# Zeroing a cache gradient: one zero region split between a memory-to-memory copy and a store, and one zero store issued earlier

## The chip, the cores and the metric

The kernel runs on one core of one Trainium2 chip. The metric is the device time of one execution in microseconds (us); lower is better. Five engines work side by side in a core: PE (TensorE, matrix multiplication), DVE (VectorE), ACT (ScalarE), POOL (GpSimd) and SP (SyncE). SP computes nothing; here it issues nearly all transfers. Transfers are carried by the core's 16 DMA engines, each of which works through its own share of every transfer, in the order in which SP issued them.

## What is computed

It is the forward pass and all gradients of a small decoding block: four tokens, one attention layer that looks at the last 1024 positions of a 4096-position key and value cache, and a feed-forward layer, added together. Cut to what matters here:

```python
def _A_ref(x, k_cache, v_cache, wq, wo):
    W = min(4096, max(256, Sk // 4))            # 1024
    k = jnp.repeat(k_cache[:, :, Sk - W:, :], rep, axis=1)
    v = jnp.repeat(v_cache[:, :, Sk - W:, :], rep, axis=1)
    scores = jnp.einsum("bhqd,bhkd->bhqk", q, k) * (Dh ** -0.5)
    o = jnp.einsum("bhqk,bhkd->bhqd", _softmax(scores), v)
    ...
return x + _A_ref(xn, ...) + _B_ref(xn, ...)    # and its vjp with grad_out
```

The outputs are the result, the gradient of x, the gradients of the two caches (`out_2` for keys, `out_3` for values, each 4 x 8 x 4096 x 128 in bf16) and the gradients of the five weight matrices. Only the last 1024 of the 4096 positions of a cache take part, so the first 3072 positions (`K0`) of both cache gradients are zero. They still have to be written: two tensors of 4 batches x 8 kv-heads x 3072 x 128 x 2 bytes, 768 KB for each kv-head, 48 MB in all.

## The kernel before

The kernel loads the feed-forward weights, does the feed-forward forward and backward passes, and then goes through the attention in four groups `t` of two kv-heads each (`NT` = 4). A group loads its part of the two caches and of the two attention weights, builds scores and probabilities (`kv_steps`, `softmax`, `softmax_d`), and leaves behind gradient pieces: `stg_dv` and `stg_dk` for the caches (1 MB each, two of each in a group), `osb_o` and `osb_q` for the weights (512 KB each, two of each in a group). The pieces (functions `dvdk` and `dw`) are put in a list `bg`, and `tick` takes them out between the matrix multiplications of the main line, so the pieces of group t are made while group t+1 runs. Each piece ends in a call of `store` (line 100), which puts one DMA on SP's queue.

The zeros come from `ztile`, a tile in on-chip memory (128 rows of 12 KB) that is set to zero once. `zlist` (line 159) holds 32 regions, each of two neighbouring kv-heads of one batch of one tensor; the last one belongs to `out_3`. `zero(n)` (line 161) takes the next n of them and stores `ztile` to each: 1.5 MB in 128 rows of 12 KB. Calls of `zero` are strewn over the program by hand: after the cache-gradient stores (line 490), after some of the feed-forward stores, at the start of the attention part, and a batch of four in the last group (line 734). What is left in the list when all is issued is stored at line 755.

SP issues everything in program order and stands at each DMA until what it stores has been written by DVE or ACT. Besides, a DMA waits until the one eight places before it in the order has landed, since eight completion semaphores are used in turn. `store` says that gradient stores and zero stores write disjoint bytes, so they don't wait for one another on that ground. The tiles that hold gradient pieces are used in turn too: three of the kind `stg`, four of the kind `osb`; DVE and ACT can only refill one when its last store has landed.

Of the kernel before, what the change touches and what calls it, by code (L numbers as in the profile page):

```python
# [14 lines left out]
P = 128  # L15
# [3 lines left out]
def kernel(  # L19
# [28 lines left out]
    nc = tc.nc  # L48

    B, Sq, D = A_x.shape  # L50
    _, G, Sk, Dh = A_k_cache.shape
# [4 lines left out]
    K0 = Sk - W  # L56
    F = B_w_gate.shape[1]
    ND = D // P
    NF = F // P
    GP = 2  # L60
    NT = G // GP
# [27 lines left out]
    def evac(out, in_, n, half=False, eng=None):  # L89

        eng = "dve" if half else eng
        ca, cd = (190 + n) / 1.2, (120 + (n / 2 if half else n)) / 0.96
        if eng is None:
            eng = "act" if load["act"] + ca <= load["dve"] + cd else "dve"
        load[eng] += ca if eng == "act" else cd
        if eng == "act":
            return nc.scalar.copy(out=out, in_=in_)  # L97
        return nc.vector.tensor_copy(out=out, in_=in_)  # L98

    def store(eng, out, in_, kind):  # L100

        eng.nop()
        d = eng.dma_start(out=out, in_=in_)
        for k in ("rest", "zeros") if kind == "rest" else ("rest",):
            tc.declare_no_dep(d.ins, group=k, reason="stores write disjoint parts of the outputs")
        tc.add_to_no_dep_group(kind, d.ins)
        return d
# [12 lines left out]
    def load_w(t, eng=nc.gpsimd):  # L120
        pool = w_pool[t % 2]
        wo_t[t] = pool.tile([P, HG, D], BF16, name="wo_sb", tag="wo")
        eng.dma_start(out=wo_t[t][:], in_=wo_v[t])
        wq_t[t] = pool.tile([P, ND, CW], BF16, name="wq_sb", tag="wq")
        eng.dma_start(out=wq_t[t][:], in_=wq_v[t])
# [32 lines left out]
    ztile = const.tile([P, ZW], BF16, name="ztile")  # L158
    zlist = deque((og, b, g) for b in range(B) for g in range(0, G, ZR) for og in (out_2, out_3))

    def zero(n=1):
        for _ in range(min(n, len(zlist))):
            og, b, g = zlist.popleft()
            store(nc.sync, og[b, g:g + ZR, 0:K0, :].rearrange("g (m j) d -> m g (j d)", m=P // ZR), ztile[:], "zeros")


    nc.gpsimd.memset(ztile[:], 0.0)
# [94 lines left out]
    def tick(n):  # L262
        for _ in range(min(n, len(bg))):
            bg.popleft()()
# [3 lines left out]
    def link(n=1):  # L268
        for _ in range(min(n, len(chain))):
            chain.popleft()()  # L270
# [227 lines left out]
    def dw(t):  # L498
        o_s, dq_r = st[t]["os"], st[t]["dq"]

        def piece_o(g, i, held):
            if i == 0:
                held["osb"] = outp.tile([P, rep, D], BF16, name="osb_o", tag="o")
            mps = ps_w.tile([P, D], FP32, name="dwo_ps", tag="w")
            nc.tensor.matmul(mps[:], lhsT=o_s[:, g].rearrange("p r d -> p (r d)")[:, i:rep * Dh:rep], rhs=dyr[:],  # L505
                             start=True, stop=True)
            evac(held["osb"][:, i, :], mps[:], 512)
            if i == rep - 1:
                r0 = (t * HG + g * rep) * Dh
                store(nc.sync, out_5[r0:r0 + rep * Dh, :].rearrange("(p i) n -> p (i n)", i=rep),  # L510
                      held["osb"][:].rearrange("p i n -> p (i n)"), "rest")

        def piece_q(c2, k, held):
            if k == 0:
                held["osb"] = outp.tile([P, 2, GP, rep, Dh], BF16, name="osb_q", tag="o")
            ci, i2 = k // 2, k % 2
            c = c2 * 2 + ci
            mps = ps_w.tile([P, 2, GP, Dh], FP32, name="dwq_ps", tag="w")
            for i in range(2):
                nc.tensor.matmul(mps[:, i].rearrange("p g d -> p (g d)"), lhsT=xnm[:, i2 * 2 + i, c * P:(c + 1) * P],  # L520
                                 rhs=dq_r[:].rearrange("p g d -> p (g d)"), start=True, stop=True)
            evac(held["osb"][:, ci, :, i2 * 2:(i2 + 1) * 2, :], mps[:].rearrange("p i g d -> p g i d"), 512)
            if k == 3:
                store(nc.sync, out_4[c2 * 2 * P:(c2 + 1) * 2 * P, t * CW:(t + 1) * CW].rearrange("(c p) j -> p c j", p=P),
                      held["osb"][:].rearrange("p c g i d -> p c (g i d)"), "rest")

        assert rep == 4
        made = []
        for g in range(GP):
            held = {}  # L530
            made.append([lambda g=g, i=i, held=held: piece_o(g, i, held) for i in range(rep)])
        for c2 in range(ND // 2):
            held = {}
            made.append([lambda c2=c2, k=k, held=held: piece_q(c2, k, held) for k in range(4)])
        return made
# [181 lines left out]
    with tc.tile_pool(name="kv_b", bufs=GP, reuse_waits="tile") as kv_b, \  # L717
            tc.tile_pool(name="w_b", bufs=1, reuse_waits="tile") as w_b, \
            tc.tile_pool(name="stage", bufs=3, reuse_waits="tile") as stage:
        kv_pool[1], w_pool[1] = kv_b, w_b  # L720
        zero()
        pre(0)
        load_w(1)
        load_kv(1, 0)
        for t in range(NT):
            kv_steps(t, 0, 0)
            if t == 0:
                zero()
                load_kv(1, 1)
                zero()  # L730
            softmax(t)
            kv_steps(t, 1, 1)
            if t == NT - 1:
                zero(4)
            link(len(chain))
            softmax_d(t)
            link()
            odq(t, 0)
            load_kv(t + 2, 1)
            if t + 1 < NT:  # L740
                pre(t + 1)
            link(len(chain))
            odT(t, 0)
            odq(t, 1)
            load_kv(t + 2, 0)
            tick(2)
            odT(t, 1)
            fin(t)
            if t + 2 < NT:
                load_w(t + 2)  # L750
            (k0, k1), (o0, o1, q0, q1) = dvdk(t, 1), dw(t)
            for p in (k0, o0, k1, o1, q0, q1):
                bg.extend(p)
        tick(len(bg))
        zero(len(zlist))

        fin_ps = []
        for o in range(2):
            f_ps = ps_w.tile([B, ND, P], FP32, name="f_ps", tag="w")
            for c in range(ND):  # L760
                nc.tensor.transpose(f_ps[:, c, :], acc[:, o, c, :], ident_f[:])
            fin_ps.append(f_ps)
        acc_o = fin_ps[0][:].rearrange("b c p -> b (c p)")
        acc_d = attw.tile([B, P, ND], FP32, name="acc_d", tag="P_s")
        nc.vector.tensor_copy(out=acc_d[:].rearrange("b p c -> b c p"), in_=fin_ps[1][:])
        acc_d = acc_d[:].rearrange("b p c -> b (p c)")
        out_b = attw.tile([B, D], BF16, name="out_b", tag="pT")
        nc.vector.tensor_tensor(out=out_b[:], in0=acc_o, in1=x4[:], op=ALU.add)
        nc.scalar.dma_start(out=out_0.rearrange("b s d -> (b s) d"), in_=out_b[:])

        s1 = attw.tile([B, 1], FP32, name="s1", tag="m")
        nc.vector.reduce_sum(out=s1[:], in_=acc_d, axis=AX.X)
        pr = attw.tile([B, D], FP32, name="pr", tag="dS_s")
        s2 = attw.tile([B, 1], FP32, name="s2", tag="es")
        nc.vector.tensor_tensor_reduce(out=pr[:], in0=acc_d, in1=xn_f[:], scale=1.0, scalar=0.0,
                                       op0=ALU.mult, op1=ALU.add, accum_out=s2[:])
        nm1 = attw.tile([B, 1], FP32, name="nm1", tag="rr")
        nc.vector.tensor_scalar(out=nm1[:], in0=s1[:], scalar1=-1.0 / D, scalar2=None, op0=ALU.mult)
        nm2 = attw.tile([B, 1], FP32, name="nm2", tag="gs")
        nc.vector.tensor_scalar(out=nm2[:], in0=s2[:], scalar1=-1.0 / D, scalar2=None, op0=ALU.mult)  # L780
        nc.vector.scalar_tensor_tensor(out=pr[:], in0=xn_f[:], scalar=nm2[:, 0:1], in1=acc_d,
                                       op0=ALU.mult, op1=ALU.add)
        nc.vector.tensor_scalar(out=pr[:], in0=pr[:], scalar1=nm1[:, 0:1], scalar2=rstd[:, 0:1],
                                op0=ALU.add, op1=ALU.mult)
        dx_b = attw.tile([B, D], BF16, name="dx_b", tag="E_f")
        nc.vector.tensor_tensor(out=dx_b[:], in0=pr[:], in1=dy4[:], op=ALU.add)
        nc.scalar.dma_start(out=out_1.rearrange("b s d -> (b s) d"), in_=dx_b[:])
# [30 lines left out]
```

## Time and profile before

| | |
|---|---|
| median of 3 runs | 282.91 us (282.87 to 283.6) |
| the profiled execution, its own time | 283.0 us |
| span of that execution in the profile | 281.0 us |
| busy: PE / DVE / ACT / POOL | 203.1 / 164.1 / 117.8 / 40.1 us |
| moved by DMA | 112.12 MB, 30.68 MB read from memory and 81.01 MB written |
| zero stores | 32 of 1536 KB, 18.1 us from issue to landing in the middle |
| `stg_dv` and `stg_dk` stores | 8 and 8 of 1024 KB, 13.0 and 20.8 us to landing |

The span runs from the first to the last recorded event of the core; the time of the execution is 2.0 us longer. "Busy" is the time in which an engine had an instruction in work. In a table by stretches of time, the column "DMA share" gives the mean busy share of the 16 DMA engines: 1.00 is all of them all the time (it can read a little over 1 where neighbouring packets overlap in the records), and 0.06 is one of them alone. "From issue to landing" counts from SP's instruction until the last of a transfer's bytes is in place, so it holds the time that the transfer stands behind earlier ones.

### The profile page before, as it was taken

How to read it: one execution, taken by the hardware profiler on the slowest of the kernel's cores; microseconds unless marked ns; L12 is line 12 of the kernel's file. 1: busy time of each engine (PE TensorE's matmuls, PEld its weight loads, DVE VectorE, ACT ScalarE, POOL GpSimd, SP SyncE). 2: the span in 40 equal slices, each digit the busy share in tenths (PEclk: the TensorE clock that was granted, in tenths of full speed). 3: DMA queues.
4: the chain of work that ended last, by engine and by line, in shares of the span. 5: the costliest groups of instructions: out<-in, count | busy, mean ns of one | idle time of the engine just before them, and what ended most of it. 6: DMA issues, size and time to landing. Idle time of an engine off the chain costs nothing.

```text
span 281.0 us, 6867 instructions
## 1 busy us (share of the span) xinstructions
PE 203.1 (72%) x2972; PEld 138.8 (49%) x2972; DVE 164.1 (58%) x313; ACT 117.8 (42%) x219; POOL 40.1 (14%) x40
## 2 busy tenths in 40 slices
PE   0276699959789889998999299898999599390000
PEld 0265476735456665566775156677556484140000
DVE  7946646645776655577666067767677728386000
ACT  2030386635035418764448056443866038370000
POOL 8600000007002150002250000223000400000000
PEclk9999589986999999999999969999999979977555
DMA  7999999999999999999999999999999999999990
GB/s 264 393 375 431 431 426 417 425 419 424 369 395 424 422 420 420 426 415 422 419 417 411 412 424 423 431 383 398 385 368 415 387 432 410 425 429 422 398 422 30
DMA packets 19565, 112.12 MB, mean 399 GB/s; under 512 B 1664, under 2 KB 4496, under 8 KB 11088
## 3 DMA queue, kind: packets, MB, share of 16 engines
q1 hardware_dynamic: 17744, 103.56, 89.6%
q0 software_dynamic: 1632, 6.29, 5.6%
q10 hardware_dynamic: 160, 1.84, 1.9%
q8 instruction: 23, 0.38, 0.5%
q14 instruction: 6, 0.05, 0.0%
HBM read 30.68 MB, written 81.01 MB: 397 GB/s over the span
## 4 chain that ended last, share of the span: by engine, by line
PE 47%; DMA 22%; DVE 16%; ACT 4%; issue 2%; SPq 0%; DVEq 0%; ACTq 0%
DMA out_dram<-stg_dv 13%; PE T_ps L279 8%; PE kv_ps L484 7%; DMA wd_sb<-in_B_w_down_dram 6%; PE S_ps L345 5%; PE od_ps L450 5%; DMA out_dram<-osb_g 4%; DVE T_sb L98 3%; DVE dS_s L367 2%; PE wdT_ps L279 2%; PE dwq_ps L520 2%; PE acc_ps L256 2%; PE dwd_ps L660 2%; DVE P_s L367 2%; PE wgT_ps L279 2%
## 5 line engine op out<-in xcount | busy, mean ns | idle before, releaser
L98 DVE COPY T_sb<-T_ps 128x1024 bf16<-128x1024 bf16 x64 | 44.1, 688 | 26.7 <-PE T_ps L279 26.5
L97 ACT CAST stg_dk<-kv_ps 128x512 bf16<-128x512 f32 x52 | 29.2, 588 | 31.2 <-PE kv_ps L484 12.4
L97 ACT CAST stg_dv<-kv_ps 128x512 bf16<-128x512 f32 x51 | 28.1, 588 | 24.9 <-PE kv_ps L484 24.3
L484 PE MATMUL kv_ps<-qmr,dS_s 128*128 128x512 bf16 x64 | 23.9, 414 | 11.3 <-ACT stg_dk L97 10.6
L463 POOL TENSOR_TENSOR o_s<-od_r,msk_r 128x512 bf16<-128x512 bf16 x8 | 9.1, 1157 | 110.2 <-DVE od_r L455 80.9
L484 PE MATMUL kv_ps<-domr,P_s 128*128 128x512 bf16 x64 | 21.3, 382 | 0.0
L279 PE MATMUL T_ps<-ident,vb 128*128 128x128 bf16 x256 | 20.3, 225 | 0.4 <-DVE T_sb L98 0.4
L279 PE MATMUL T_ps<-ident,kb 128*128 128x128 bf16 x256 | 20.4, 225 | 0.0
L279 PEld LDWEIGHTS <-kb 128*128 128x128 bf16 x256 | 17.5, 101 | 4.5 <-issue 1.3
L279 PEld LDWEIGHTS <-vb 128*128 128x128 bf16 x256 | 17.2, 101 | 5.0 <-issue 3.2
L97 ACT CAST osb_q<-dwq_ps 128x512 bf16<-128x512 f32 x25 | 14.6, 587 | 8.3 <-PE dwq_ps L520 7.4
L329 POOL TENSOR_TENSOR domr<-r,msk 128x1024 bf16<-128x1024 bf16 x4 | 7.6, 1892 | 71.2 <-DVE r L326 65.1
L97 ACT CAST osb_g<-dwg_ps 128x512 bf16<-128x512 f32 (+1 forms) x25 | 12.3, 544 | 12.3 <-PE dwg_ps L673 6.3
L97 ACT CAST osb_o<-dwo_ps 128x512 bf16<-128x512 f32 x24 | 13.9, 586 | 4.5 <-PE dwo_ps L505 2.9
L98 DVE CAST stg_dk<-kv_ps 128x512 bf16<-128x512 f32 x12 | 8.0, 688 | 12.0 <-DMA out_dram<-stg_dv 11.2
L98 DVE COPY wgT<-wgT_ps 128x1024 bf16<-128x1024 bf16 x14 | 9.6, 686 | 6.8 <-PE wgT_ps L279 6.8
L345 PE MATMUL S_ps<-T_sb,qm 128*32 128x256 bf16 x128 | 12.7, 387 | 0.6 <-DVE T_sb L98 0.5
L345 PE MATMUL S_ps<-T_sb,dom 128*32 128x256 bf16 x128 | 12.7, 388 | 0.1
L505 PE MATMUL dwo_ps<-dyr,o_s 128*128 128x512 bf16 x32 | 12.4, 413 | 0.3 <-ACT stg_dk L97 0.2
L98 DVE COPY woT<-woT_ps 128x1024 bf16<-128x1024 bf16 x16 | 11.0, 686 | 2.7 <-PE woT_ps L279 2.3
L484 PEld LDWEIGHTS <-dS_s 128*128 128x128 bf16 x64 | 6.2, 101 | 12.2 <-issue 11.1
L520 PE MATMUL dwq_ps<-od_r,xnm 128*128 128x256 bf16 x64 | 11.6, 274 | 0.3 <-ACT osb_q L97 0.2
(188 smaller groups left out, 385.0 us busy)
## 6 DMA issues: line engine op xcount, KB each, us to landing
out_dram<-ztile SPq DMA_DIRECT2D x32, 1536.0 KB, 18.1
kb<-in_A_k_cache_dram SPq DMA_DIRECT2D x8, 1024.0 KB, 17.4
vb<-in_A_v_cache_dram SPq DMA_DIRECT2D x8, 1024.0 KB, 20.7
out_dram<-stg_dv SPq DMA_DIRECT2D x8, 1024.0 KB, 13.0
out_dram<-stg_dk SPq DMA_DIRECT2D x8, 1024.0 KB, 20.8
out_dram<-osb_o SPq DMA_DIRECT2D x8, 512.0 KB, 17.4
out_dram<-osb_q SPq DMA_DIRECT2D x8, 512.0 KB, 13.8
out_dram<-osb_g SPq DMA_DIRECT2D x8, 448.0 KB, 14.3
```

Source lines behind the costliest of these rows:

```text
L97: return nc.scalar.copy(out=out, in_=in_)
L98: return nc.vector.tensor_copy(out=out, in_=in_)
L256: nc.tensor.matmul(ps[:, c, :], lhsT=lf(c), rhs=rhs, start=(k == 0), stop=(k == len(terms) - 1))
L279: nc.tensor.transpose(ps[:, i, :], a, ident[:])
L329: nc.gpsimd.tensor_tensor(out=mr[:].rearrange("p g q d -> p (g q) d"), in0=r4[:, k, :].unsqueeze(1).broadcast_to([P, SL, Dh]), in1=msk[:]. ...
L345: nc.tensor.matmul(ps[b * RB:(b + 1) * RB, :], lhsT=zt[:, b * GP + g, c0:c0 + RB], rhs=T_sb[:].rearrange("p (x b) -> p b x", b=B)[:, b, :] ...
L367: nc.vector.scalar_tensor_tensor(out=out[:], in0=src[:].unsqueeze(2).broadcast_to([P, WQ, B]), scalar=rr[:, 0:1], in1=mskb[:].unsqueeze(1) ...
L450: nc.tensor.matmul(od_ps[g * 32:g * 32 + B * rep, k, g, :], lhsT=cols[:, jj, g * NQ + q, :], rhs=blks[(t, g)][:, j, :], start=(j == 0), st ...
L463: nc.gpsimd.tensor_tensor(out=o_s[:, g], in0=rows[:, g].unsqueeze(1).broadcast_to([P, rep, Dh]), in1=msk_r[:].unsqueeze(2).broadcast_to([P ...
L484: nc.tensor.matmul(mps[:].rearrange("p q d -> p (q d)"), lhsT=src[:, j * P:(j + 1) * P], rhs=mr[:, g].rearrange("p q d -> p (q d)"), start ...
L505: nc.tensor.matmul(mps[:], lhsT=o_s[:, g].rearrange("p r d -> p (r d)")[:, i:rep * Dh:rep], rhs=dyr[:], start=True, stop=True)
L520: nc.tensor.matmul(mps[:, i].rearrange("p g d -> p (g d)"), lhsT=xnm[:, i2 * 2 + i, c * P:(c + 1) * P], rhs=dq_r[:].rearrange("p g d -> p ...
```

## The change

The batch of four zero stores in the last group becomes two zero stores and a call of `zero_4`, which does the last region of `zlist`. Of that region's two kv-heads, `zero_4` copies the first from `out_2[0, 0]`, whose zeros were the first to be written, directly from memory to memory; this transfer is laid out as 4 rows of four contiguous pieces of 24576 elements (48 KB). The second kv-head is stored from `ztile` as 128 rows of 6 KB. (The branch `k0 < K0` is empty with these sizes.) The fourth store of the batch moves: it is now issued in group 1, the second of the four, right behind the last `osb_q` store of that group's weight gradients. The order of SP's other DMAs is the same, and so are the instructions of the other engines.

```diff
+    def zero_4():
+
+        og, b, g = zlist.pop()
+        assert og is out_3
+        k0 = 4 * K0 // 4
+        d_, s_ = (x[0:k0, :].rearrange("(c m j) d -> m c (j d)", m=4, c=4) for x in (og[b, g], out_2[0, 0]))
+        store(nc.sync, d_, s_, "zeros")
+        if k0 < K0:
+            w = (K0 - k0) // P
+            store(nc.sync, og[b, g, k0:K0, :].rearrange("(m j) d -> m (j d)", m=P), ztile[:, 0:w * Dh], "zeros")
+        w = K0 // P
+        store(nc.sync, og[b, g + 1, 0:K0, :].rearrange("(m j) d -> m (j d)", m=P), ztile[:, 0:w * Dh], "zeros")
@@ in dw(t), piece_q(c2, k, held), behind the store of osb_q @@
+                zero(t == NT - 3 and c2 == ND // 2 - 1)
@@ in the loop over the groups t @@
             if t == NT - 1:
-                zero(4)
+                zero(2)
+                zero_4()
```

## The prediction

> **What bounds the kernel now.** I read the page's first lines, the queue table, then a table of busy time by stretches, because the first lines leave no room for an engine as the bound: PE is busy 72% of the span, the DMA row is full nearly from end to end.
>
> ```profile
> span 281.0 us, 6867 instructions
> PE 203.1 (72%) x2972; PEld 138.8 (49%) x2972; DVE 164.1 (58%) x313; ACT 117.8 (42%) x219; POOL 40.1 (14%) x40
> DMA  7999999999999999999999999999999999999990
> ...
> q1 hardware_dynamic: 17744, 103.56, 89.6%
> ...
> q8 instruction: 23, 0.38, 0.5%
> ```
>
> The reader is to see the DMA row: nines, and a 0 in the last slice, though the span isn't over there. The last 7 us have DMA work, but hardly any. The table by stretches (us from the start of the span; DMA share and GB/s are the last two columns) takes that apart and also shows where the DMA engines ran dry earlier:
>
> ```profile
> 150.00:186.00 36.00, 28.18 (x374) 18.37 (x371) 21.62 (x37) 16.06 (x30) 2.03 (x2) 0.91 1.01 422
> 186.80:188.40 1.60, 1.52 (x41) 1.28 (x42) 1.35 (x6) 0.74 (x3) 0.24 (x1) 1.00 0.79 314
> 188.40:194.30 5.90, 5.55 (x114) 4.27 (x108) 3.70 (x9) 2.47 (x5) 3.50 (x2) 1.00 1.01 413
> 194.30:195.10 0.80, 0.41 (x12) 0.31 (x13) 0.48 (x1) 0.00 (x0) 0.00 (x0) 1.00 0.83 333
> ...
> 201.10:202.60 1.50, 1.50 (x19) 0.84 (x18) 1.31 (x3) 0.68 (x3) 0.00 (x0) 1.00 0.54 221
> ...
> 209.80:211.20 1.40, 1.40 (x18) 0.98 (x17) 0.67 (x3) 1.26 (x4) 0.00 (x0) 1.00 0.48 187
> ...
> 219.70:220.40 0.70, 0.70 (x32) 0.70 (x28) 0.00 (x0) 0.00 (x0) 0.00 (x0) 1.00 0.62 219
> 220.40:264.00 43.60, 23.77 (x247) 13.93 (x241) 24.42 (x45) 15.56 (x29) 3.02 (x2) 0.83 1.01 420
> ...
> 274.50:275.50 1.00, 0.00 (x0) 0.00 (x0) 0.00 (x0) 0.00 (x0) 0.00 (x0) 0.50 0.15 61
> 275.50:279.50 4.00, 0.00 (x0) 0.00 (x0) 0.00 (x0) 0.00 (x0) 0.00 (x0) 0.50 0.06 25
> ```
>
> Two things. First, from 275.5 to 279.5 the share is 0.06: one DMA engine of 16 works alone, at 25 GB/s. By the packet records twelve engines end at 274.1 to 274.4, three at 274.6 to 275.2, and one at 279.6, 5.4 us late; the span ends 1.4 us after it. So the end is set by one DMA engine, the late one, and not by the sum of bytes. Second, there are five holes between 186 and 221. Multiplying (1 - share) by length gives 0.34 + 0.14 + 0.69 + 0.73 + 0.27 = 2.2 us of idle time as a mean over the engines. The share never drops under 0.48, and in the records at least four engines work through every hole: the late one doesn't rest there.
>
> The issue times of SP (start, duration) say what the holes are:
>
> ```profile
> 174.87 3.01 SPq L103 DMA_DIRECT2D out_dram<-osb_q  x2
> 186.84 0.55 SPq L103 DMA_DIRECT2D out_dram<-stg_dv  x1
> 187.44 0.59 SPq L103 DMA_DIRECT2D out_dram<-ztile  x1
> ...
> 216.54 3.15 SPq L103 DMA_DIRECT2D out_dram<-osb_q  x2
> 219.74 4.40 SPq L103 DMA_DIRECT2D out_dram<-ztile  x4
> ```
>
> From 177.9 to 186.8 SP issues nothing, as it waits for the next gradient piece; what was queued runs out, and the later holes are the same on a smaller scale.
>
> **What the Trainium skill says.** "DMA: Bandwidth & Descriptors", section "Why a DMA increments its semaphore by 16 and not by 1", says that a transfer goes over k DMA engines, the largest number up to 16 that divides the slowest dimension of both sides, and that the hardware queues take the lowest-numbered k. So 128 rows give 16 engines and 4 rows give engines 0 to 3. The trace agrees on the number: each of the two 4-row loads at the start leaves four completion packets in the records, each large transfer 16. The same page, "Specifications", gives about 27 GiB/s for one engine; here a 12288-byte zero packet takes 0.46 us, 26.7 GB/s. No page that I found prices a direct memory-to-memory copy, and no transfer of before is one.
>
> **Is the late engine one of the four?** I decided no. The two small 4-row stores near the end (`out_b`, `dx_b`) run on four engines. In the records each of the four `dx_b` packets is followed by a packet of 0.47 to 0.53 us, the length of a 12288-byte one, while the late engine is then sending `stg_dk` packets of 8192 bytes, 0.31 us each. The four end at 274.2 to 274.4, with the twelve. What makes the late one late I only infer: the 23 instruction-fetch packets (16 KB each) share engines with the stores.
>
> **The change part by part.** *The moved store.* It costs an engine the same 8 packets of 0.46 = 3.7 us, only earlier: SP can issue it at 178, where it stands idle for 8.9 us. It waits for the DMA eight places back, a `stg_dk` store issued at 154.8; at 20.8 us that lands near 176, so nothing queued behind is delayed. It fills the first hole and leaves a backlog that fills the others: an engine that stood through all five gains up to 3.7 us, one that stood only in the last three about 2.3 (0.36 + 0.98 + 0.95, the idle time divided over the twelve that rest). The late engine gains nothing. Later landings could stall DVE and ACT on an `stg` tile; the first `stg_dv` of group 2 is issued at 186.8 and its buffer is wanted about 202, so I put this at nothing; without that cover, up to 1 us of compute that ends at 258, well ahead of the stores.
>
> *The split region.* It removes 96 KB (3.66 us) from every engine. The 128-row half gives back 8 packets of 6 KB, half of it, 1.83 us. The copy adds nothing on twelve engines, and on engines 0 to 3 a row each: 192 KB, 16 packet lengths of 0.457 = 7.3 us at the rate of the stores. Sum for the twelve, the late one among them: -1.83 us. For engines 0 to 3: -3.66 + 1.83 + 7.3 = +5.5 us. The copy is not in the trace, so bounds: 7.3 us is the engine's known rate; below it nothing is gained, since the late engine sets the end. Above: if reading and writing memory had to share what an engine moves, 14.6 us. I take 7.3, since loads from memory (1 MB `kb`, 8192 bytes in 0.31 us) and stores to it run at the same rate, and each alone fills the engine's own path.
>
> *The end.* Late engine: 279.6 - 1.8 = 277.8. Engines 0 to 3: 274.3 + 5.5 - (2.3 to 3.7) = 276.1 to 277.5. The others end near 271. The late engine still ends last, by a little; span 281.0 - 1.8 = 279.2, time 283.0 - 1.8 = 281.2. The profiled execution is 0.1 above the median of the runs, so 281.1. The cover is thin: with the copy at 8.0 us or more, engines 0 to 3 take over the end; at 10 us the gain is used up.
>
> *Queues and waits.* The number of SP's DMAs rises by one, under 1 us of issue where SP waits anyway. The source of the copy was stored around 18.5 and is long there. The compute wait that matters late,
>
> ```profile
> ACT stg_dk L97 <- DMA out_dram<-stg_dv: 11.6, 2, 7.0
> ```
>
> ends at 245.4 when the late engine has its share of `stg_dv` down; it moves 1.8 us earlier with it.
>
> **Rivals.** *Half rate (slower).* Mechanism: the direct copy uses an engine twice, so engines 0 to 3 need 14.6 us: 274.3 - 3.66 + 1.83 + 14.6 - 3 = 284.1 against 279.6, time 287.5. It decides from about 10 us per row on. For it: the trace has no such transfer, and both ends press on the same memory. Against: 48 KB pieces are the longest here, and memory is moving only about 420 GB/s by loads and stores mixed without loss. *No change.* The holes aren't filled on engines 0 to 3, or just the last one (0.36 us): 274.3 + 5.5 - 0.4 = 279.4, time 282.7; the same comes from a copy at about 10 us with holes filled. For it: the holes depend on compute, which may slip with the backlog. Against: the backlog of 3.7 us is larger than the 2.2 us of holes. *The late engine is one of the four.* Then it gets +5.5: 288.5; the packet records speak against it, and it goes with the slower cases.
>
> **How the numbers follow.** The forecast, late engine 1.8 us earlier: 0.66, own range 280.4 to 282.0. No change: 0.12. Slower: 0.22, mostly 286 to 289. A measurement of this kernel can tell about 0.3% (0.85 us) from no change, so faster 0.66, same 0.12, slower 0.22. Range: from 280.4 to 286.5, which takes in the first two and the milder part of a slow copy, and leaves out under 2 in 10, the full half rate.
>
> **What would show it.** The share-0.06 tail of one engine should be gone, or replaced by about four engines (0.25) for at most 1 us; the holes at 186 to 221 filled; copy packets of 48 KB should take 1.8 us each. Wrong would be: copy packets of 3 us or more, a tail at share 0.25 of several us (engines 0 to 3 last), or the same lone engine ending where it did.

## The result and the profile after

The changed kernel takes 281.69 us in the median against 283.36 us for the kernel before, 20 runs of each. The ratio is 0.9935 with a 95% interval of 0.9924 to 0.9947, so 1.8 us faster (0.65% of 283.4 us; interval 1.5 to 2.2 us); the two medians lie 1.7 us apart. The profiled execution has a span of 279.3 us against 281.0.

From the page of the changed kernel, the lines that answer to those of before:

```profile
span 279.3 us, 6868 instructions
PE 202.7 (73%) x2972; PEld 138.3 (50%) x2972; DVE 164.1 (59%) x313; ACT 117.4 (42%) x219; POOL 40.1 (14%) x40
DMA  7999999999999999999999999999999997999992
...
q1 hardware_dynamic: 17764, 103.56, 90.2%
...
q8 instruction: 23, 0.38, 0.5%
```

PE, DVE, ACT and POOL are as busy as before to within 0.4 us, and SP's queue moves the same 103.56 MB in 20 packets more. The difference is in when the bytes are moved and on which DMA engine. The table by stretches of the changed kernel (length first, DMA share and GB/s last) covers the holes of before, a later stretch and the end:

```profile
186.80:188.40 1.60, 1.52 (x29) 0.90 (x28) 1.45 (x6) 1.13 (x3) 0.00 (x0) 1.00 1.06 430
...
194.30:195.10 0.80, 0.26 (x5) 0.11 (x2) 0.80 (x2) 0.00 (x0) 0.00 (x0) 1.00 1.07 451
...
201.10:202.60 1.50, 1.50 (x20) 0.91 (x17) 1.00 (x2) 1.03 (x2) 0.00 (x0) 1.00 1.02 429
...
209.80:211.20 1.40, 1.40 (x15) 0.90 (x15) 0.94 (x3) 1.01 (x3) 0.00 (x0) 1.00 0.79 325
...
219.70:220.40 0.70, 0.70 (x32) 0.70 (x28) 0.27 (x2) 0.00 (x0) 0.00 (x0) 1.00 0.96 366
...
231.00:235.50 4.50, 4.43 (x66) 2.98 (x65) 3.75 (x7) 3.16 (x7) 0.00 (x0) 1.00 0.58 245
...
273.00:276.00 3.00, 0.00 (x0) 0.00 (x0) 0.00 (x0) 0.00 (x0) 0.00 (x0) 0.50 0.33 139
276.00:277.00 1.00, 0.00 (x0) 0.00 (x0) 0.00 (x0) 0.00 (x0) 0.00 (x0) 0.50 0.26 111
277.00:278.00 1.00, 0.00 (x0) 0.00 (x0) 0.00 (x0) 0.00 (x0) 0.00 (x0) 0.50 0.03 12
```

In the kernel before, the first five stretches were at 0.79, 0.83, 0.54, 0.48 and 0.62; three of the holes are gone and two are shallower. The lone engine of before (0.06 for 4 us) has company: a share of 0.33 from 273 to 276 is about five engines. By the packet records four of them end at 276.8 to 277.0 and the last one at 277.9; in the kernel before it ended at 279.6. The hole from 231 to 235.5 is new. In the kernel before this stretch reads

```profile
231.00:235.50 4.50, 4.44 (x61) 2.77 (x59) 3.57 (x8) 3.17 (x7) 0.00 (x0) 1.00 0.96 404
```

SP's issues show where the stores went:

```profile
175.26 3.01 SPq L103 DMA_DIRECT2D out_dram<-osb_q  x2
179.44 0.67 SPq L103 DMA_DIRECT2D out_dram<-ztile  x1
187.22 0.55 SPq L103 DMA_DIRECT2D out_dram<-stg_dv  x1
...
220.13 2.25 SPq L103 DMA_DIRECT2D out_dram<-ztile  x2
222.43 1.33 SPq L103 DMA_DIRECT2D out_dram<-out_dram  x1
223.80 1.25 SPq L103 DMA_DIRECT2D out_dram<-ztile  x1
```

The moved store stands alone in the time in which SP used to wait for the next gradient piece, and that piece (`stg_dv`) is issued at 187.2 as against 186.8.

### The profile page after: what moved, and what is told of

It reads as the page before. It is cut to its first block, busy times and chain, and to the rows that moved or that the text cites. A ratio compares the mean times of both kernels' runs of the same rounds, so it can differ in the third digit from the quotient of the medians.

```text
span 279.3 us, 6868 instructions
## 1 busy us (share of the span) xinstructions
PE 202.7 (73%) x2972; PEld 138.3 (50%) x2972; DVE 164.1 (59%) x313; ACT 117.4 (42%) x219; POOL 40.1 (14%) x40
## 3 DMA queue, kind: packets, MB, share of 16 engines
q1 hardware_dynamic: 17764, 103.56, 90.2%
## 4 chain that ended last, share of the span: by engine, by line
PE 46%; DMA 22%; DVE 17%; ACT 4%; issue 2%; SPq 1%; DVEq 0%; ACTq 0%
DMA out_dram<-stg_dv 12%; PE T_ps L292 8%; PE kv_ps L497 6%; DMA wd_sb<-in_B_w_down_dram 6%; PE S_ps L358 6%; PE od_ps L463 5%; DMA out_dram<-osb_g 4%; DVE T_sb L98 3%; DVE dS_s L380 2%; PE dwq_ps L533 2%; PE acc_ps L269 2%; PE dwd_ps L674 2%; DVE P_s L380 2%; PE wgT_ps L292 2%; PE pT_ps L292 2%
## 5 line engine op out<-in xcount | busy, mean ns | idle before, releaser
L497 PE MATMUL kv_ps<-qmr,dS_s 128*128 128x512 bf16 x64 | 23.2, 399 | 8.9 <-ACT stg_dk L97 8.2
L518 PE MATMUL dwo_ps<-dyr,o_s 128*128 128x512 bf16 x32 | 11.8, 388 | 0.5 <-DVE stg_dk L98 0.2
L98 DVE COPY wqT<-wqT_ps 128x1024 bf16<-128x1024 bf16 x16 | 10.6, 685 | 1.8 <-PE wqT_ps L292 1.6
```

The lines of the kernel that those rows point to most:

```text
L497: nc.tensor.matmul(mps[:].rearrange("p q d -> p (q d)"), lhsT=src[:, j * P:(j + 1) * P], rhs=mr[:, g].rearrange("p q d -> p (q d)"), start ...
```

## The experiments

The theory: one DMA engine, not among engines 0 to 3, falls behind the others and sets the end; the 4-row copy takes 48 KB (1.8 us) from it, and the moved store makes room on engines 0 to 3, which take over the load. The main rivals: filling the holes brings the gain; a copy from memory is cheaper than a store from on-chip memory; the bytes as a whole count, whichever engine carries them. Every kernel was timed against the kernel before on the same chip; a difference in us below is the ratio less 1, times 283 us. The diffs are against the changed kernel where nothing else is said, and `...` marks what is left out.

### The moved store alone

```diff
-                zero(2)
-                zero_4()
+                zero(3)
```

> The zero store of group 1 is moved as in the change; the split region is stored as in the kernel before. Theory (one late DMA engine sets the end and never rests in the holes): no gain, 0.0 us with 0.4 either way; the tail at a DMA share of 0.06 stays, and the twelve engines ahead of it end 2 to 3 us earlier, so it gets longer. Rival (filling the holes brings the gain): about 1.7 us faster.

Ratio 0.9999 (0.9987 to 1.0012): 0.0 us. Its table by stretches, one hole of before and the end:

```profile
186.80:188.40 1.60, 1.44 (x27) 0.86 (x29) 1.20 (x4) 1.38 (x4) 0.00 (x0) 1.00 1.04 421
...
274.00:279.00 5.00, 0.00 (x0) 0.00 (x0) 0.00 (x0) 0.00 (x0) 0.00 (x0) 0.50 0.06 27
```

The hole is filled, and nothing comes of it: the lone tail is 5 us long, as fifteen engines are done by 274.1 and the late one ends at 279.8. The twelve leading engines ended only 1 us earlier than before, not the 2 to 3 expected.

### The split alone

```diff
-                zero(t == NT - 3 and c2 == ND // 2 - 1)
...
-                zero(2)
+                zero(3)
                 zero_4()
```

> The split region (4-row copy and 128-row half) as in the change, no zero store moved. Theory: the late engine still loses 1.8 us, but engines 0 to 3 get 5.5 us more and no hole to make up for it, so they end near 279.8 in the place of the late engine: 0.0 us with 0.5 either way, with a tail at a share near 0.25. Rival (the split alone brings the gain and the moved store is idle): 1.7 us faster.

Ratio 1.0013 (1.0002 to 1.0024): 0.4 us slower, within what the theory gave. The end of its table:

```profile
276.00:279.00 3.00, 0.00 (x0) 0.00 (x0) 0.00 (x0) 0.00 (x0) 0.00 (x0) 0.50 0.30 127
279.00:280.00 1.00, 0.00 (x0) 0.00 (x0) 0.00 (x0) 0.00 (x0) 0.00 (x0) 0.50 0.12 49
```

Four engines end together, at 279.7 to 279.9, and the late engine is done 2 us ahead of them. So neither part gains by itself: the split shortens the late engine and makes four others as late as it was, and the moved store is what those four need to be 2.8 us earlier.

### The same copy over 16 engines

```diff
-        d_, s_ = (x[0:k0, :].rearrange("(c m j) d -> m c (j d)", m=4, c=4) for x in ...)
+        d_, s_ = (x[0:k0, :].rearrange("(c m j) d -> m c (j d)", m=16, c=1) for x in ...)
```

> The change with its copy laid out as 16 rows of one 48 KB piece, so that each of the 16 DMA engines carries one piece: the same bytes, the same source, no shift of load between engines. Theory: the late engine has the load it had before, so 0.0 us with 0.4 either way and a long tail at 0.06. Rival (a copy from memory is cheaper than a store from on-chip memory, or fewer packets are): the gain of the change, 1.7 us, stays.

Ratio 1.0002 (0.9984 to 1.0019): 0.1 us. The tail is that of the kernel before:

```profile
274.00:279.00 5.00, 0.00 (x0) 0.00 (x0) 0.00 (x0) 0.00 (x0) 0.00 (x0) 0.50 0.06 27
```

The bytes, the source and the piece size are those of the change, and all of the gain is gone. It isn't the copy that is cheap; it is where it runs.

### How much is taken from the late engine, and given to the four

Half of the kv-head on 4 rows, the other half in 128 rows:

```diff
-        k0 = 4 * K0 // 4
+        k0 = 2 * K0 // 4
```

> The change with half of the kv-head copied on 4 rows (two 24 KB steps of each row's load are gone: four pieces of 24 KB) and the other half stored in 128 rows. Theory: the late engine loses half of what it lost, 0.9 us; engines 0 to 3 get 2.7 us instead of 5.5 and end near 274, far ahead. So 0.9 us faster than before, with the lone tail back. Rival (any unloading of the shared path brings the whole gain): 1.7 us faster.

Ratio 0.9972 (0.9958 to 0.9987): 0.8 us faster. Both kv-heads on 4 rows:

```diff
-        k0 = 4 * K0 // 4
-        d_, s_ = ...
-        store(nc.sync, d_, s_, "zeros")
...
-        w = K0 // P
-        store(nc.sync, og[b, g + 1, 0:K0, :]...
+        for h in range(2):
+            d_, s_ = (x[0:K0, :].rearrange("(c m j) d -> m c (j d)", m=4, c=4) for x in (og[b, g + h], out_2[0, 0]))
+            store(nc.sync, d_, s_, "zeros")
```

> Both kv-heads of the region copied on 4 rows, no 128-row half. Theory: the late engine loses 3.7 us, but engines 0 to 3 get 10.9 us more than before and set the end near 282.3: 2.7 us slower than before, with 0.5 either way, and a tail at 0.25 of about 9 us. Rival (engines 0 to 3 have more room than the one-region count says, or two copies overlap): at most 1 us slower, or faster.

Ratio 1.0082 (1.0054 to 1.011): 2.3 us slower. The end of the two tables, first the half, then the double:

```profile
274.50:278.50 4.00, 0.00 (x0) 0.00 (x0) 0.00 (x0) 0.00 (x0) 0.00 (x0) 0.50 0.06 28
```

```profile
275.00:281.00 6.00, 0.00 (x0) 0.00 (x0) 0.00 (x0) 0.00 (x0) 0.00 (x0) 0.50 0.25 109
```

With half the shift the lone engine is last, at 278.8; with twice the shift four engines are, alone for 6 us (about 9 were expected) and until 281.3 to 281.7. The shift of the change stands between: the late engine ends at 277.9, the four at 276.8 to 277.0. The last of the four has 0.84 us to spare, and a whole shift brings the two groups 7.3 us nearer (5.5 more for the four, 1.8 less for the late one). So about a ninth more would bring both together and gain some 0.2 us; that is an estimate, and less than these runs can tell from nothing.

### Which engine is the late one?

By the Trainium skill, "DMA: Bandwidth & Descriptors" (section "Why a DMA increments its semaphore by 16 and not by 1"), a copy of r rows runs on engines 0 to r-1. The records agree on the number: the copy leaves r completions for each r tried here, so only a transfer that goes over all 16 engines has a share for each of them. If the late engine is among them it gets 768/r KB in the place of 48 KB. So r was raised from 4 in separate kernels:

```diff
-        d_, s_ = (x[0:k0, :].rearrange("(c m j) d -> m c (j d)", m=4, c=4) for x in ...)
+        d_, s_ = (x[0:k0, :].rearrange("(c m j) d -> m c (j d)", m=8, c=2) for x in ...)
```

> The change with its copy laid out as 8 rows of two 48 KB pieces, so on engines 0 to 7. This asks where the late engine is. If among 8 to 15: it loses 1.8 us as in the change, 1.7 us faster than before, and engines 0 to 7 end about 2 us ahead of it (their load grows by 1.8 us only, so nothing stands at a share of 0.25 near the end). If among 4 to 7: it gains 1.8 us of load, and the time is 1.8 us above before. Rival (no late engine, the sum of bytes counts): as the change, whatever the rows.

Ratio 1.0054 (1.0034 to 1.0075): 1.5 us slower. For 7, 6 and 5 rows the same line has `m=7, c=2`, `m=6, c=4` and `m=5, c=4`; where 3072 positions don't divide, the few left over have a store of their own.

> The copy of the one kv-head laid out as 7 rows of two 54.75 KB pieces, on engines 0 to 6; the 6 positions left over (1.5 KB) in a small store of their own. The 8-row copy put the late engine among 4 to 7. If it is engine 7: it loses 1.8 us, engines 0 to 6 get only 2.4 us, and the time is 1.8 us below before. If it is 4, 5 or 6: it gets 2.4 us more, and the time is 2.4 us above before.

Ratio 1.009 (1.0067 to 1.0113): 2.5 us slower.

> The copy of the one kv-head laid out as 6 rows of four 32 KB pieces, on engines 0 to 5. The 7-row copy put the late engine among 4, 5 and 6. If it is 6: it loses 1.8 us, engines 0 to 5 get 3.0 us and stay ahead: 1.8 us faster than before. If it is 4 or 5: it gets 3.0 us, and the time is 3.0 us above before.

Ratio 1.0117 (1.0092 to 1.0142): 3.3 us slower.

> The copy of the one kv-head laid out as 5 rows of four 38.25 KB pieces, on engines 0 to 4, the 12 positions left over (3 KB) in a small store of their own. The 6-row copy put the late engine at 4 or 5. If it is 5: it loses 1.8 us, engines 0 to 4 get 4.0 us and end near 275.4: 1.8 us faster than before, with room for more. If it is 4: 4.0 us more on it, less what a copy of other sizes showed, so 3.5 to 4.5 us slower than before, and four rows is the only low row count that spares it.

Ratio 1.0149 (1.0132 to 1.0166): 4.2 us slower. The end of the 5-row kernel's table:

```profile
279.00:283.00 4.00, 0.00 (x0) 0.00 (x0) 0.00 (x0) 0.00 (x0) 0.00 (x0) 0.50 0.06 28
283.00:284.00 1.00, 0.00 (x0) 0.00 (x0) 0.00 (x0) 0.00 (x0) 0.00 (x0) 0.50 0.03 12
```

The lone engine is still the last, now at 283.8. The fewer the rows, the slower, until at 4 the sign turns. Worked out from the share, at 26.7 GB/s, the late engine should get 1.8, 2.4, 3.1 and 4.0 us; the runs show 1.5, 2.5, 3.3 and 4.2. Under the rule that the page states, the late engine is number 4, and a low row count that spares it must be 4 or less. That the numbering is the page's isn't shown by a run; that the late engine carries data at 5, 6, 7 and 8 rows and none at 4 is. It can be seen in the copy's own completions too: at 4 rows all come within 0.3 us; at 5, 6, 7 and 8 rows the last comes 8.0, 4.7, 5.4 and 6.3 us after the one before it.

Both kv-heads on 7 rows, as a try for more:

> Both kv-heads of the region copied on 7 rows each. If the late engine is 7: it loses 3.7 us and ends near 276.0; engines 0 to 6 get 4.9 us, less the holes, and end near 276.3: 3.3 us faster than before and 1.6 faster than the change, both groups ending together. If it is 4, 5 or 6: 4.9 us slower than before. Rival (the change has taken what there is, another bound follows): no better than the change.

Ratio 1.0166 (1.0137 to 1.0195): 4.7 us slower, as the sum has it for a late engine under 7 (4.9 us).

### Why is it late?

To the kernel before, behind its last transposes:

```diff
+        w_ps = ps_w.tile([P, ND * B], FP32, name="w_ps", tag="w")
+        for _ in range(384):
+            nc.tensor.matmul(w_ps[:], lhsT=ztile[0:1, 0:P], rhs=ztile[0:1, 0:ND * B], start=True, stop=True)
```

> The kernel before with 384 further pairs of weight load and small matmul (1 row, 16 columns) behind the last transposes, when PE has nothing left to do; their results go nowhere. They are 768 instructions more for PE, about 3 instruction-fetch packets of 16 KB on top of 23. If the late engine is late because it fetches PE's instructions: each of the 23 costs it about 0.4 us (its 5.4 us at the end and 3 to 4 us that the others rest in the holes, over 23), so 1.0 to 1.8 us slower, the tail at 0.06 longer by that. If it is late for another reason: 0.0 us, since PE ends long before the stores.

Ratio 1.0051 (1.0033 to 1.0069): 1.4 us slower. From its queue table, and from its timeline (start, duration, engine, in brackets the idle time before):

```profile
q8 instruction: 26, 0.43, 0.6%
```

```profile
261.10 3.56 PE L765 MATMUL w_ps<-ztile 1*128 1x16 bf16 x128 [3.15 <-issue]
...
268.12 1.96 PE L765 MATMUL w_ps<-ztile 1*128 1x16 bf16 x68 [3.46 <-issue]
```

There are three instruction-fetch packets of 16 KB more, 26 against 23. PE's extra work ends at 270.1, 11 us before the stores do, so no store waits for it. The tail grows:

```profile
276.00:281.00 5.00, 0.00 (x0) 0.00 (x0) 0.00 (x0) 0.00 (x0) 0.00 (x0) 0.50 0.06 27
281.00:282.00 1.00, 0.00 (x0) 0.00 (x0) 0.00 (x0) 0.00 (x0) 0.00 (x0) 0.50 0.03 12
```

The late engine ends at 281.6 as against 279.6. So instructions of PE make this engine late. That it is their fetch, as the expectation had it, the records speak against:

- A fetch packet takes 0.88 to 1.12 us in these two kernels. In the kernel before, seven of them run between 176 us and the end. The late engine sent each of its transfers in that time with at most 0.64 us lost (a zero store took it 3.6 to 4.3 us, where its 8 packets back to back need 3.66), less than one fetch packet lasts. So none of the seven held it up.
- In this run the three packets more start at 258.7, 265.8 and 273.0. The lateness (the last of a transfer's 16 completions less their middle) of the store that landed at 256.1 was already 0.5 us above that of the same store in the kernel before. The third packet added nothing: while it ran, the late engine sent 2 KB packets every 0.08 us without a break, and another engine stopped between two 12 KB packets.

What the late engine's loss follows is PE at work. It lost 1.07 us in the transfers that cover the first 188 pairs, 0.60 us in the next ones with 128 pairs, and 0.33 us in the one with the last 68: about 5 ns for a matmul with its weight load. When PE has nothing left to do, in the kernel before from 258 on, it sends a zero store in 3.62 to 3.68 us like the rest. For the 2972 matmuls of the kernel 5 ns each would make some 15 us, an estimate; it catches up where the others run dry. What it is about these instructions that takes time from one DMA engine stays open. Each execution on record, the timed ones too, was recorded with its span and clock, and no run shows whether the recording has a part in it.

## Why the prediction was right

It forecast 281.1 us, 1.8 us below the median it started from; measured were 1.8 us by the ratio. The median itself is 281.7, as the kernel before, too, was 0.45 us slower in these runs than in the three that the forecast started from (283.36 against 282.91). The steps, one by one.

The bound was read correctly from the tail at a share of 0.06: the kernel waits for one DMA engine. That the late engine isn't one of the four, decided from the lengths of the packets behind the small `dx_b` stores, holds: on 4 rows it is relieved, on 5 it isn't. Why it is late the prediction only inferred, from the fetch packets, and that inference fails; nothing in its sum rests on it.

The late engine: forecast to end at 277.8, it ended at 277.9. The rate of the copy, which nothing in the kernel before showed and for which the bounds were 7.3 and 14.6 us a row: the 48 KB packets took 1.82 us at the shortest and 1.83 in the middle. One or two of each row's four took longer (up to 2.35 us), so a row took 7.6 to 7.8 us from first to last, more than the 7.3 of the sum, and not far from the 8.0 at which the prediction had the four engines take over the end. The half-rate rival is out; it would have ended four engines some 7 us later than they did.

Engines 0 to 3: forecast 276.1 to 277.5, measured 276.8 to 277.0. The moved store gave them 2.8 us (the change against the split alone), within the 2.3 to 3.7 forecast. Without the moved store, forecast from the same sum, 279.8; measured 279.7 to 279.9. The "no change" rival (holes not filled for these four) is what the split alone does.

One term was wrong, with no effect on the time. The prediction had the other engines end near 271; they ended at 272.9 to 274.0. It took it that the holes would be filled for good. But with one zero store fewer in the batch of group 3, and less to carry for the twelve that have no share in the copy, these run dry from 231 to 235.5, where SP has nothing to issue until `stg_dv` at 234.0; (1 - 0.58) times 4.5 us is 1.9 us of idle time in the mean. Engines 0 to 3 have the copy to work on in that time and the late engine its arrears, so the hole costs nothing. The moved store alone shows the same in part: its share from 231 to 235.5 is 0.77, and its leading engines gained 1 us, not 2 to 3. One sign was also named amiss: four engines near the end were to be seen for at most 1 us. By the prediction's own end times they had to be at work for 5 us or more after the rest, and it was 3 to 4. The moved store, forecast for 178, was issued at 179.4, as the transfer eight places back landed only then; it did no harm.

The compute wait for `stg_dv` was to end 1.8 us earlier with the late engine. The waits of the changed kernel (us in total, times, the longest) have it at

```profile
ACT stg_dk L97 <- DMA out_dram<-stg_dv: 9.2, 2, 6.8
```

and the chain of waits lets DVE go on at 243.7, as against 245.4 before: 1.7 us.

## What to carry to other kernels

Where DMA is the bound, look at how the last few microseconds end: a share of 1/16 means that one engine is late, and then it is that engine's load that counts, not the sum of bytes, and an idle hole elsewhere is worth nothing by itself. Load can be shifted by the number of rows of a transfer, but the engines that take it over need room, and both sides have to be summed for each engine: here each part of the change gained nothing without the other. A row count is not a free choice: 4 rows gained 1.8 us, 5 rows lost 4.2.

## What was not expected of the hardware

A direct copy from memory to memory ran at the rate of a store: 49152 bytes in 1.82 us, 27.1 GB/s for an engine. It did so beside engines that stored from on-chip memory without a pause, in the split alone, where ten of the 16 packets took 1.82 to 1.85 us and the others up to 2.51:

```profile
233.00:241.00 8.00, 7.00 (x54) 2.85 (x52) 6.06 (x11) 5.74 (x11) 0.00 (x0) 1.00 1.01 413
```

And PE's instructions are paid for in a kernel that is bound by stores: 768 more, all done 11 us before the end, made it 1.4 us slower, as one DMA engine lost about 5 ns for each matmul with its weight load. PE itself stood 3.1 and 3.5 us between them, with no wait that the profile shows other than issue.
